# Linear attention into a top-1 expert layer: head tokens of k and v on 128 partitions, and the spill expert's weights through the sync queue

## The chip, the cores and the metric

The kernel runs on one core of a Trainium2 chip. The metric is the device time of one execution in microseconds (us). The engines are named as in the profile: PE (TensorE), DVE (VectorE), ACT (ScalarE), POOL (GpSimd) and SP (SyncE), which here only issues DMAs. All transfers run on the core's 16 DMA engines.

## The reference

Shapes: q, k, v are (8, 8, 576, 64) in float32 (batch, heads, tokens, head dim). The output is (4608, 512).

```python
kv = np.einsum('bhsd,bhse->bhde', k, v)
out = np.einsum('bhsd,bhde->bhse', q, kv)
rms = np.sqrt(np.mean(out * out, axis=-1, keepdims=True) + 1e-06)
attn = out / rms * g_norm                 # (b, h, s, d)

x = attn.transpose(0, 2, 1, 3).reshape(4608, 512)
logits = x @ w_gate                       # w_gate (512, 8)
expert_idx = np.argmax(logits, axis=1)
gate_w = softmax(logits)[row, expert_idx]
for e in range(8):                        # w1 (8, 512, 1024), w2 (8, 1024, 512)
    mask = expert_idx == e
    h = np.maximum(x[mask] @ w1[e], 0.0)
    out[mask] = gate_w[mask, None] * (h @ w2[e])
```

## The kernel before

Every instruction is put in order by hand: the program order of the Python code is the order on each engine.

**Attention.** For each batch b and half u (four heads), `load` (L541) issues three DMAs on SP's queue, one each for k, v and q, into tiles `mk`, `mv`, `mq` with four buffers each. The 128 partitions hold two heads of 64 token groups, and a group is nine tokens in a row, 576 numbers. `kv_mm` (L565) multiplies v and k of a head over 64 partitions, nine times, into the PSUM tile `kvps`; 64x64 pieces of the array work on different heads. `z_copy` (L583) takes `kvps` out, `fold_mm` (L588) multiplies by an identity beside the gate weights, and `x_copy` makes `kvx`. `t_mm` transposes q into `qT`. A tile step (`o_mm`, `o_red`, `o_nrm`, `o_x`) then makes 128 rows of attention output, their norm and their gate logits. After each group of tiles, `route` finds each row's expert and slot, and POOL scatters the rows (`xrow`) to `x_slots` in HBM.

The loop at L770 goes over b from 0 to 8. At step b it does the loads' consumers for batch b and the tiles of batch b - 1 (four tiles for odd b, five for even b); `load(b + 2, u)` follows the last transposes of a half.

**Experts.** `ffn` (L479) is a generator, of which `unit()` runs a step. Its groups, in order, are experts 0 to 2 with three tiles of 128 rows each, the same experts with two more tiles each, and experts 3 to 7 with five tiles each. An extra group for one tile, the spill, takes rows beyond five tiles of an expert; it stands before the last group. Which expert needs it is known only at run time. A group gathers its rows (`fetch`, POOL), transposes them (`xpose`), does `stage1` (w1 and relu, into `hT`) and `stage2` (w2), evicts to `y` on DVE (L351, three buffers), and scatters `y` to the output on POOL (L354). For further spill tiles a loop at the end (L837) runs a number of times that the data decide.

**Weights.** An expert's weights come in eight parts of 512 KB in float32 on SP's queue into `wst` (four buffers), and DVE casts each to float16 (`w_cast`, L204). `w_step` (L211) casts the oldest part once four are staged, then loads the next. Experts 0 to 2 may be loaded during attention (`EARLY`); the others only once the attention's memory is free (`late["pool"]`). During attention `w_step` is called twice for each b from 1 (L799) and once per tile from b = 6 (L814); in `ffn`, four times in the first stage of each group but the spill, and once for each tile of the second. The spill's weights come in another way: `dyn_group.fetch` (L380) issues twelve indirect gathers on POOL (L403) that cast on the way, by row numbers that `dyn_tables` (L421) has made on DVE.

## Time and profile before

| | |
|---|---|
| median of 3 runs | 376.94 us (373.69 to 377.51) |
| profiled execution | 376.71 us, span 374.9 us |
| granted PE clock, mean | 0.842 |
| PE busy | 292.8 us (78%) |
| DVE / ACT / POOL busy | 173.8 / 121.3 / 144.9 us |
| moved by DMA | 83.76 MB, mean 223 GB/s |
| SP's queue (q1) | 61.87 MB, 26368 packets |
| POOL's queue (q0) | 21.06 MB, 8704 packets |

The profile is of one execution. Busy shares are averages over the stages, which have different limits, so they are read stage by stage; the page cuts the span into 40 slices for that. A digit in a row of slices is the busy share in tenths. In an answer on waits, the first name is the engine that was idle, the arrow points at what released it, and the numbers are the total in us, how often, and the longest. In the chain and in the timeline, a line is the start in us, the length in us, the engine, the operation and the line of code.

### The profile page before, as it was taken

What the parts mean: (1) busy time and instruction counts of PE and PEld (TensorE: products, weight loads), DVE (VectorE), ACT (ScalarE), POOL (GpSimd) and SP (SyncE); (2) the same over time, 40 slices, a digit from 0 to 9 for tenths busy, and PEclk for the clock granted to TensorE, in tenths of its full rate; (3) what the DMA queues carried; (4) which work ended last, traced back from release to release, by engine and by line L of the source; (5) the groups of instructions that cost most, each with busy time, mean ns of one, the idle gap of its engine ahead of it and who ended that gap; (6) DMA issues with size and microseconds to landing.
All of it is one profiled execution on the core that took longest, in us unless ns stands there. A gap on an engine that the chain in (4) does not pass through costs nothing.

```text
span 374.9 us, 8180 instructions
## 1 busy us (share of the span) xinstructions
PE 292.8 (78%) x3271; PEld 202.8 (54%) x3271; DVE 173.8 (46%) x424; ACT 121.3 (32%) x324; POOL 144.9 (39%) x151
## 2 busy tenths in 40 slices
PE   2687879597948989347999979788986687998990
PEld 2476777385836778236454546445552353655640
DVE  0136355258517567576377655668701402324130
ACT  1346444155414443132431233314051041232510
POOL 7000003600352103475564447735577375413031
PEclk9999578679665566755899998989999898999996
DMA  8999999569762755582479999976528425302021
GB/s 242 391 391 392 393 395 357 215 215 376 267 255 63 206 171 198 171 250 89 141 226 394 384 388 389 373 283 224 200 78 134 132 75 70 143 28 102 3 84 50
DMA packets 36759, 83.76 MB, mean 223 GB/s; under 512 B 5740, under 2 KB 7021, under 8 KB 36720
## 3 DMA queue, kind: packets, MB, share of 16 engines
q1 hardware_dynamic: 26368, 61.87, 46.3%
q0 software_dynamic: 8704, 21.06, 17.9%
q8 instruction: 26, 0.43, 0.5%
q10 hardware_dynamic: 1648, 0.29, 0.5%
q14 instruction: 13, 0.11, 0.1%
HBM read 71.77 MB, written 15.50 MB: 233 GB/s over the span
## 4 chain that ended last, share of the span: by engine, by line
PE 45%; issue 16%; DMA 13%; DVE 11%; another core or an unknown queue 5%; ACT 4%; POOL 3%; POOLq 1%; ACTq 0%; SPq 0%; DVEq 0%
PE ops L634 11%; PE hp L330 11%; PE yp L346 8%; PE kvps L576 7%; DMA wst<-in_moe_w_dram 6%; PE tps L559 4%; POOL out_dram L354 3%; DMA mv<-in_v_dram 3%; DVE ms L647 2%; ACT sq L643 2%; PE xps L310 2%; DVE y L351 2%; DMA g<-in_g_norm_dram 2%; DVE xsT L313 1%
## 5 line engine op out<-in xcount | busy, mean ns | idle before, releaser
L338 ACT ACTIVATE hT<-hp 128x320 f16<-128x320 f32 (+3 forms) x136 | 53.5, 427 | 127.6 <-PE hp L330 105.5
L330 PE MATMUL hp<-xsT,w1e 128*128 128x320 f16 (+2 forms) x512 | 78.4, 308 | 11.7 <-DVE xsT L313 6.5
L346 PE MATMUL yp<-w2e,hT 128*128 128x512 f16 x320 | 79.0, 396 | 8.9 <-DVE y L351 5.5
L354 POOL DMA_INDIRECT out_dram<-y,idv x40 | 43.0, 1076 | 79.6 <-DVE y L351 64.9
L330 PEld LDWEIGHTS <-w1e 128*128 128x128 f16 x512 | 51.3, 100 | 38.8 <-issue 19.2
L634 PE MATMUL ops<-kvx,qT 64*128 64x72 f32 (+1 forms) x640 | 54.7, 339 | 4.4 <-issue 2.4
L346 PEld LDWEIGHTS <-hT 128*128 128x128 f16 x328 | 32.1, 102 | 43.6 <-issue 13.0
L726 POOL DMA_INDIRECT x_slots<-xrow,posi x36 | 36.3, 1007 | 46.2 <-issue 25.4
L634 PEld LDWEIGHTS ops<-kvx,qT 64*128 64x128 f32 (+1 forms) x640 | 48.3, 242 | 9.6 <-issue 4.8
L576 PE MATMUL kvps<-mk,mv 64*64 64x64 f32 x1152 | 35.4, 273 | 23.1 <-issue 12.6
L351 DVE TENSOR_SCALAR y<-yp,xl 128x512 f32<-128x512 f32 x40 | 29.9, 748 | 36.6 <-PE yp L346 29.1
L647 DVE TENSOR_REDUCE ms<-sq 128x8 f32<-128x512 f32 x36 | 24.7, 685 | 45.1 <-ACT sq L643 35.9
L576 PEld LDWEIGHTS kvps<-mk,mv 64*64 64x64 f32 x1152 | 29.5, 180 | 28.3 <-issue 27.3
L313 DVE TENSOR_SCALAR xsT<-xps,g 128x512 f16<-128x512 f16 x41 | 19.2, 477 | 45.1 <-PE xps L310 27.5
L643 ACT ACTIVATE sq<-ops 128x512 f32<-128x512 f32 x36 | 21.5, 598 | 51.6 <-PE ops L634 41.4
L276 POOL DMA_INDIRECT xl<-x_slots,idxa x31 | 32.8, 1058 | 9.4 <-issue 7.9
L693 POOL COPY xrow<-tokc 128x3 int32<-128x3 int32 x12 | 2.3, 193 | 76.3 <-DVE xrow L659 75.0
L559 PE MATMUL tps<-ctile,mq 128*128 128x128 f32 x144 | 29.3, 342 | 2.1 <-ACT qT L560 1.9
L659 DVE TENSOR_TENSOR xrow<-ops,rs 128x512 f16<-128x512 f32 x36 | 24.7, 686 | 8.8 <-ACT rs L652 8.6
L206 DVE CAST w1e<-wst 128x1024 f16<-128x1024 f32 x32 | 22.1, 706 | 11.6 <-DMA wst<-in_moe_w_dram 11.6
L206 DVE CAST w2e<-wst 128x1024 f16<-128x1024 f32 x32 | 22.4, 703 | 7.7 <-DMA wst<-in_moe_w_dram 5.8
L560 ACT COPY qT<-tps 128x384 f32<-128x384 f32 x48 | 22.2, 474 | 11.4 <-PE tps L559 11.3
(96 smaller groups left out, 186.2 us busy)
## 6 DMA issues: line engine op xcount, KB each, us to landing
wst<-in_moe_w_dram SPq DMA_DIRECT2D x64, 512.0 KB
mk<-in_k_dram SPq DMA_DIRECT2D x16, 576.0 KB
mv<-in_v_dram SPq DMA_DIRECT2D x16, 576.0 KB
mq<-in_q_dram SPq DMA_DIRECT2D x16, 576.0 KB
out_dram<-y,idv POOLq DMA_INDIRECT x40
x_slots<-xrow,posi POOLq DMA_INDIRECT x36
xl<-x_slots,idxa POOLq DMA_INDIRECT x31
xl<-x_slots,idxe POOLq DMA_INDIRECT x9
```

What stands on the lines that cost most here:

```text
L206: engine.tensor_copy(*w_staged.pop(0))
L276: nc.gpsimd.indirect_dma_start(out=self.xl[:, k, :], out_offset=None, in_=xs.ap(), in_offset=IndirectOffsetOnAxis(ap=idx[:, self.e, self.k ...
L330: nc.tensor.matmul(hp, self.w()[0][:, kk, f * 128 : (f + 1) * 128], self.xsT[:, kk, s : s + self.step], start=(kk == 0), stop=(kk == 3),)
L338: nc.scalar.activation(self.hT[:, f, s : s + self.step], hp, ACTF.Relu)
L346: nc.tensor.matmul(yp, self.hT[:, f, k * 128 : (k + 1) * 128], self.w()[1][:, f, :], start=(f == 0), stop=(f == 7),)
L351: nc.vector.tensor_scalar(y, yp, self.xl[:, k, D : D + 2].bitcast(F32), None, op0=ALU.mult)
L354: nc.gpsimd.indirect_dma_start(out=self.views(k), out_offset=IndirectOffsetOnAxis(ap=self.ids[:, k : k + 1], axis=0), in_=y, in_offset=Non ...
L559: nc.tensor.transpose(ps[:, c, :], src[:, 128 * m : 128 * m + 128], cv["ident"])
L576: nc.tensor.matmul(kvps[b][a][64 * y : 64 * y + 64, u, :], main["v", b, u][hs, y, cs], main["k", b, u][hs, y, cs], start=(c == 0), stop=(c ...
L634: nc.tensor.matmul(ps[p0 : p0 + 64 * n, y, o0 : o0 + 72], qT[b][hs, a, blk // 2 : blk // 2 + n, :].rearrange("d c p -> d (c p)"), kvx[b][h ...
L647: nc.vector.reduce_sum(mss[j, t], sq, axis=AXX)
L726: nc.gpsimd.indirect_dma_start(out=xs_views[9 * j + t0 + t], out_offset=IndirectOffsetOnAxis(ap=posi[:, t : t + 1], axis=0), in_=xrow[j, ( ...
```

## The change

Loads of k and v: each head is loaded by a DMA of its own (eight for k and v where there were two). A head now lies on all 128 partitions: partition p of the lower half holds tokens 9p to 9p + 4, partition 64 + p tokens 9p + 4 to 9p + 8, 320 numbers each. The token that lies in both is used once. q is loaded as before. `kv_mm` contracts over 128 partitions in four steps and over the upper 64 in a fifth, into one PSUM tile; `z_copy` is one copy in place of two.

The spill's weights are one more entry, "s", in the list of weight parts. SP reads the number of the expert from a table in SBUF into a register and loads the eight parts from there by that offset, and DVE casts them as for any other expert. The group for the loop at the end keeps the gathers.

The weight steps move: none up to b = 5, then one per tile for b = 6 and 7 and two for b = 8; in `ffn` none in the second stage of groups of experts 0 to 2, and two in the first stage of groups of two tiles. A group first loops until its own eight parts are cast. The tables for the spill are made in the fourth group, and `y` has five buffers in the groups of five tiles and in the spill.

```diff
-    w_todo = [(e, n) for e in range(E) for n in range(8)]
-    w_staged = []
+    w_todo = [(e, n) for e in [*range(E - 1), "s", E - 1] for n in range(8)]
+    spill_e = []
+    w_staged, w_done = [], {}
...
         st = P_wa.tile([128, F], F32, tag="wst", bufs=4, name=f"wst{e}_{n}")
+        if e == "s":
+            if n == 0:
+                spill_e.append(
+                    nc.values_load(
+                        tabs[0][5][0:1, 0:1], engines=(mybir.EngineType.SP,), min_val=0,
+                        max_val=E - 1,
+                        skip_runtime_bounds_check_because="the table holds the number of an expert",
+                    )
+                )
+            w1, w2 = (
+                w[bass.ds(spill_e[0], 1)].rearrange("o a b -> (o a) b") for w in (moe_w1, moe_w2)
+            )
+        else:
+            w1, w2 = moe_w1[e], moe_w2[e]
         if n < 4:
             r0 = 128 * (2 * (n % 2) + n // 2)
-            nc.sync.dma_start(st, moe_w1[e, r0 : r0 + 128, :])
+            nc.sync.dma_start(st, w1[r0 : r0 + 128, :])
             dst = w_tiles[e][0][:, n, :]
...
-        w_staged.append((dst, st))
+        w_staged.append((e, dst, st))
 
     def w_cast(engine):
         if w_staged:
-            engine.tensor_copy(*w_staged.pop(0))
+            e, dst, st = w_staged.pop(0)
+            engine.tensor_copy(dst, st)
+            w_done[e] = w_done.get(e, 0) + 1
...
-            y = self.pool().tile([128, D], F32, tag="y", bufs=3, name="y")
+            y = self.pool().tile([128, D], F32, tag="y", bufs=3 if self.small else 5, name="y")
...
-    class dyn_group(Group):
+    class SpillGroup(Group):
...
             self.tables, self.col, self.view = tables, col, view
-            self.e, self.K, self.n, self.step, self.small = E, 1, 128, 128, False
+            self.e, self.K, self.n, self.step, self.small = "s", 1, 128, 128, False
...
-        def slot_ids(self):
-            pass
...
         def fetch(self):
-            badi, xii, w1i, w2i, _ = self.tables
+            badi, xii, w1i, w2i = self.tables[:4]
...
+    class LoopGroup(SpillGroup):
+        def w(self):
+            return self.wd
+
+        def fetch(self):
+            super().fetch()
             self.wd = (
                 P_wa.tile([128, 4, F], F16, tag="w1e", bufs=3, name="w1d"),
...
-            yield
             for kk in range(12):
...
-                yield
-
-        def ready(self):
-            self.ids = late["pool"].tile([128, 1], I32, tag="d_id", name="d_id")
-            nc.vector.tensor_tensor(
-                self.ids, self.xl[:, 0, D + 2 : D + 4].bitcast(I32), self.ix[:, 13:14], op=ALU.max
-            )
+                    out_offset=None,
...
+        eti = small("d_eti", [128, T], I32)
+        nc.vector.tensor_scalar(eti, et, float(E - 1), None, op0=ALU.min)
...
+            while w_done.get(cur.e, 0) < 8:
+                w_step()
             for f in range(8):
                 cur.stage1(f)
-                if f % 2 == 1 and real >= 0:
+                if f % 2 == 1 if cur.K != 2 else f % 4 == 1:
                     w_step()
...
-                if f == 2 and cur.e == EARLY:
+                if f == 2 and real == EARLY:
                     tabs.append(dyn_tables())
-                if f == 0 and cur.e == EARLY + 1:
-                    spill = dyn_group(tabs[0], slice(0, 1), out_views[E * SLOT_TILES])
-                    weights = spill.fetch()
+                if f == 3 and cur.e == EARLY + 1:
+                    spill = SpillGroup(tabs[0], slice(0, 1), out_views[E * SLOT_TILES])
+                    spill.fetch()
                     order.insert(len(order) - 1, spill)
-                if cur.e > EARLY:
-                    next(weights, None)
...
-            if cur.e == E - 2:
-                for _ in weights:
-                    pass
-                spill.ready()
...
-                if real >= 0:
+                if not cur.small:
                     w_step()
...
 
         def load(b, u):
-            for n, src in (("k", k), ("v", v), ("q", q)):
-                t = PA.tile([128, 2, 576], F32, tag=f"m{n}", bufs=4, name=f"m{n}{b}{u}")
-                nc.sync.dma_start(
-                    t,
-                    src[b, 4 * u : 4 * u + 4].rearrange("(i a) (p c) d -> (a p) i (c d)", a=2, c=9),
-                )
+            for n, src in (("k", k), ("v", v)):
+                t = PA.tile([128, 4, 320], F32, tag=f"m{n}", bufs=4, name=f"m{n}{b}{u}")
+                for i in range(4):
+                    head = src[b, 4 * u + i]
+                    nc.sync.dma_start(
+                        t[:, i, :],
+                        bass.AP(
+                            tensor=head.tensor, offset=head.offset,
+                            ap=[[256, 2], [576, 64], [1, 320]],
+                        ),
+                    )
                 main[n, b, u] = t
+            t = PA.tile([128, 2, 576], F32, tag="mq", bufs=4, name=f"mq{b}{u}")
+            nc.sync.dma_start(
+                t, q[b, 4 * u : 4 * u + 4].rearrange("(i a) (p c) d -> (a p) i (c d)", a=2, c=9)
+            )
+            main["q", b, u] = t
...
         def kv_mm(b, u):
             if u == 0:
-                kvps[b] = [
-                    PSA.tile([128, 2, 64], F32, tag="KV", bufs=2, name=f"kvps{b}{a}")
-                    for a in range(2)
-                ]
-            for c in range(9):
-                cs = slice(64 * c, 64 * c + 64)
-                for y in range(2):
-                    for a in range(2):
-                        hs = slice(64 * a, 64 * a + 64)
+                kvps[b] = PSA.tile([128, 4, 64], F32, tag="KV", bufs=2, name=f"kvps{b}")
+            for a in range(2):
+                for c in range(5):
+                    hs = slice(64 if c == 4 else 0, 128)
+                    cs = slice(64 * c, 64 * c + 64)
+                    for y in range(2):
                         nc.tensor.matmul(
-                            kvps[b][a][64 * y : 64 * y + 64, u, :],
-                            main["v", b, u][hs, y, cs],
-                            main["k", b, u][hs, y, cs],
-                            start=(c == 0), stop=(c == 8),
+                            kvps[b][64 * y : 64 * y + 64, 2 * u + a, :],
+                            main["v", b, u][hs, 2 * y + a, cs],
+                            main["k", b, u][hs, 2 * y + a, cs],
+                            start=(c == 0), stop=(c == 4),
                         )
 
         def z_copy(b):
-            zs[b] = PA.tile([128, 2, 2, 64], F32, tag="z", bufs=2, name=f"z{b}")
-            for a in range(2):
-                nc.scalar.copy(zs[b][:, a], kvps[b][a])
+            zs[b] = PA.tile([128, 4, 64], F32, tag="z", bufs=2, name=f"z{b}")
+            nc.scalar.copy(zs[b], kvps[b])
...
                 xrow[j, t // 3] = PA.tile(
-                    [128, 3, ROW], I16, tag="xrow", bufs=5, name=f"xrow{j}{t}"
+                    [128, 3, ROW], I16, tag="xrow", bufs=4, name=f"xrow{j}{t}"
...
                         if x % 3 == 2:
                             if b + 2 < B:
                                 load(b + 2, x // 3)
-                            if b > 0:
-                                w_step()
...
-                if b >= B - 2:
+                for _ in range((0, 1, 1, 2)[max(b - 5, 0)]):
                     w_step()
```

## The prediction

> **What bounds the kernel now.** I read four views, in this order: the page, for the shape of the span; the DMA view of one stretch, for what the queues can carry; the waits, for who is late; the chain with its times, for where each stage ends.
>
> The page first.
>
> ```profile
> span 374.9 us, 8180 instructions
> ...
> PEclk9999578679665566755899998989999898999996
> DMA  8999999569762755582479999976528425302021
> GB/s 242 391 391 392 393 395 357 215 215 376 267 255 63 206 171 198 171 250 89 141 226 394 384 388 389 373 283 224 200 78 134 132 75 70 143 28 102 3 84 50
> ...
> q1 hardware_dynamic: 26368, 61.87, 46.3%
> q0 software_dynamic: 8704, 21.06, 17.9%
> ...
> q10 hardware_dynamic: 1648, 0.29, 0.5%
> ```
>
> Each slice is 9.4 us. The DMA engines are full twice: up to about 65 us, when k, v and q stream in, and from about 195 to 245 us, when the expert weights do. Between them TensorE is the limit, at a granted clock of five to seven tenths. The DMA view of 10 to 60 us prices the full stretch:
>
> ```profile
> DMA packets 8622, 19.62 MB, mean 392 GB/s; under 512 B 540, under 2 KB 540, under 8 KB 8613
> ...
> q1 hardware_dynamic: 8613, 19.49, 103.8%
> ```
>
> So 16 engines move 392 GB/s, 24.5 GB/s each, and one engine moves its packets without gaps from one DMA to the next (103.8% of the stretch). Now the waits, first of all engines, then of SP's queue:
>
> ```profile
> PE kvps L576 <- DMA mv<-in_v_dram: 10.3, 3, 7.3
> ```
> ```profile
> SPq L544 <- PE kvps L576: 24.4, 6, 10.6
> ```
>
> TensorE waits for k and v only three times, all at the start. Later SP waits for TensorE: the loads run ahead and are held back by their four buffers. The chain gives the ends of the stages:
>
> ```profile
> 143.01 2.13 PE kvps L576 x72
> ...
> 173.80 0.76 DVE xsT L313 x2
> ...
> 176.33 2.72 PE hp L330 x8
> ```
> ```profile
> 289.20 3.50 another core or an unknown queue
> 292.73 0.76 DVE y L351
> ```
>
> The last kv product starts at 143 us, although SP issued its loads by 98 us; the first expert matmul starts at 176.3. That leaves 374.9 - 176.3 = 198.6 us for the experts. The second fence of the chain is one of the places where the expert stage stalls: an eviction to y (three buffers) waits for something that the chain can't name. I read it as the scatter that would free the buffer, which stands on POOL's queue behind the spill group's weight gathers (seven of the twelve are issued from 281 to 288 us).
>
> [...]every DMA of q1 has 128 partitions outermost on both sides, and rows (48 x 256 for k, v, q; 32 x 128 and 32 x 256 for the weights: 24,576) plus 16 completions for each of 112 issues (1,792) make the 26,368 packets of the page. No DMA of the kernel before has a smaller outer dimension[...].
>
> **The change part by part.**
>
> *Loads of k and v.* The pattern before merges heads and token groups into one dimension of 128. The new one, per head, is [[256, 2], [576, 64], [1, 320]]: the outer dimension is 2, since a step of 256 can't merge with 64 steps of 576. [...]Per engine a head is 64 rows of 1,280 bytes. The price of such a row: at 24.5 GB/s, 52 ns; by a line through two rows of the page, q1 (46.3% of 16 x 374.9 us over 26,368 packets = 105 ns for 2,346 bytes) and q10 (0.5%: 18 ns for 176 bytes), 62 ns. I take 56, nearer the first, because packets overlap a little when an engine is full (the 103.8%). [...]There are 8 x 8 heads of k and as many of v: 128 x 64 = 8,192 rows on each of the two engines, 459 us[...]. Behind them in the same queue stand q's rows: 16 loads x 16 rows x 94 ns (2,304 bytes at 24.5 GB/s) = 24 us. POOL's scatters of x share the two engines: about 24 of 36 come before the end, 132 KB / 16 = 8.3 KB at 123 ns per 2.4 KB (q0) = 0.42 us each, 10 us. With 2 us before the first issue moves data, the last of k, v, q lands at 2 + 459 + 24 + 10 = 495 us, where before it was needed at 143. SP issues nine DMAs for three, 96 more at about 0.4 us: 38 us on SP, beside 459 of transfer, nothing. Bytes go up by a ninth (320 for 288); that is in the row price.
>
> *The kv products.* 16 calls of 72 records become 40 records on 128 rows. At full clock 72 took 1.28 us (chain, 18.90 us), four 64x64 tiles at once; on 128 rows only two can go at once, so one call costs 0.7 (same time per record) to 1.4 us (twice). At most 9 us gained or 2 lost over the kernel, and all of it lies beside the loads: nothing. The same holds for one copy of z in place of two and the row buffers of four for five.
>
> *Weight steps.* Before, 14 steps (two for each b from 1) and then one per tile from b = 6, 28 in all, which is enough for all 24 loads of the early experts. After: none up to b = 5, then 5 + 4 + 10 = 19. On SP they now stand behind the last k, v, q, so the first arrives at about 495 us; 19 x 0.524 MB at 390 GB/s is 26 us, beside the remaining attention. The first cast (DVE, fifth step, end of b = 6) waits for that too, and evictions and reductions of b = 6 and 7 queue behind it on DVE, hence TensorE behind its two O buffers. So I count the stretch from the last kv product to the first expert matmul whole: 176.3 - 143.0 = 33 us (25, since TensorE's clock was low there before, to 45).
>
> *Experts.* POOL loses twelve gathers (0.94 to 0.96 us and 0.3 between them, 15 us); y gets five buffers; DVE gets eight casts more (0.70 us, 5.6 us in all) and SP eight loads. Casts move out of the small groups: 3 x 4 + 3 x 2 = 18 steps for 3 x 7 + 3 x 6 = 39. From the timeline, undisturbed groups take 11.5 us (three tiles), 8.3 (two), 19 (five), 6.7 (spill), and 9.4 us follow the last matmul: 3 x 11.5 + 3 x 8.3 + 5 x 19 + 6.7 + 9.4 = 171 for 198.6. Still to load are 53 of 72 parts, 28 MB, 71 us at 390 GB/s, which fits but leaves less slack in the small groups, where a group now loops until its own weights are cast. I take 180 (171 to 200). SP's new wait, for the table that names the spill expert, comes with step 57; behind it stand the spill loads and those of expert 7; the table is made in the fourth group, by step 40, so nobody waits.
>
> Sum: 495 + 33 + 180 = 708 of span, and 1.8 us around it (376.71 - 374.9): **710 us**. The profiled execution lies within 0.3 us of the median of 376.94, so no further correction. The bounds added: [...]2 + 508 + 24 + 10 + 45 + 200 + 2 = 791.
>
> **The rivals.**
>
> *Sixteen engines all the same* (the other side): the split falls on the 64 rows or on the partitions. For it: every issue before used 16[...]. Then a unit is 1.90 MB for 1.77, 4.9 us at 390 GB/s, SP's nine issues of 0.4 us fit under it, and the nine weight loads of the first 100 us (12 us of transfer) move out. Attention stays TensorE's: 174; experts 180; with 2 around it 356 us. It decides from the point where the stream takes under 143 us: 918 us of rows / k + 34, so from k = 9 up (16 in practice).
>
> *More than two, fewer than that,* or pairs that are taken in turn but don't overlap fully: at k = 4, 266 + 33 + 180 + 2 = 481 us. For it speaks only that the trace can't show the assignment.
>
> *Sixteen engines, but weights late:* 53 loads for 40 are 17 us more in a stage that was DMA-full for 50 us; if the small groups wait for all of it and the y gain is small, 377 + 17 - 9 = 385. Against it: big groups have room, 9 steps of 1.3 us in 19.
>
> **How the numbers follow.** Two engines 0.84; sixteen 0.10; between 0.03; weights late 0.03. The first case's bounds are 588 to 791; I give 600 to 790, which leaves out little of it, and with the other cases about 2 in 10. A difference of about 1% is what a measurement here tells from none. Faster: 0.10 (all of the sixteen-engine case); within 1%: 0.02, from the edges of that case and the late weights; slower: 0.88.
>
> **What would show it.** Right: the page's DMA row at 1 and 45 to 50 GB/s for two thirds of the span; q1 with 35,968 packets (34,304 rows, 2 completions for each of 128 issues, 16 for 88) in place of 37,760; kvps waiting for mv for hundreds of us; heads landing some 3.6 us apart. Experts: no L403 on POOL, and 171 to 200 us from the first hp to the end. Wrong: full DMA slices at the start and the last kvps before 150 us.

## The result: 702.0 us for 377.2 us, and the profile after

The changed kernel takes 702.04 us (median of 4 runs, 697.1 to 704.16); the kernel before, in the same comparison, 377.23 us. The ratio is 1.865, with a 95% interval of 1.8475 to 1.8825. It is slower, by nearly the amount forecast (710 us). Ratios here and below compare only runs in the faster of the two states that executions show, while medians are of all runs, so the two can differ by up to 2%. The kernel before itself took 343 to 381 us on the chips of the three sets of experiments; so times are compared only within a set, where all kernels ran on one chip.

The page of the changed kernel (each slice of its rows is 17.6 us):

```profile
span 702.4 us, 7326 instructions
...
PEclk9999999985555555555555555555579999999987
DMA  2212212212124121221312212174697665888901
GB/s 56 78 49 79 78 49 79 76 52 79 50 79 134 55 78 50 79 78 62 126 49 92 85 50 79 50 226 149 201 323 258 230 223 205 285 306 307 341 7 72
...
q1 hardware_dynamic: 35968, 68.16, 28.6%
```

Where the row of bytes began at 242 to 395 GB/s, it now begins at 49 to 79 and stays at that level, but for four slices, until 456 us, the 26th slice of 40. A DMA share of one to two tenths of 16 engines, at 49 GB/s, is two engines at the 24.5 GB/s that one of them moved before. The queue has 35,968 packets: 34,304 rows, and only two completions for each of the 128 loads of a head. TensorE is late where it never was:

```profile
PE kvps L596 <- DMA mv<-in_v_dram: 281.1, 45, 21.0
```

281.1 us of waiting for v, in 45 waits, for 10.3 us in three. SP's own timeline (start, length, operation) shows how the loads come in. These are the issues of the last half batch, and the first weights after it:

```profile
427.74 11.84 SPq L559 DMA_DIRECT2D mk<-in_k_dram  x4
439.62 13.00 SPq L559 DMA_DIRECT2D mv<-in_v_dram  x4
452.73 3.14 SPq L568 DMA_DIRECT2D mq<-in_q_dram  x1
455.91 2.62 SPq L208 DMA_DIRECT2D wst<-in_moe_w_dram  x4
```

An issue of k or v took 0.44 us before (the median; 1.6 at most); now one holds SP for 3.2 us. In the test of loads alone, below, an issue takes 3.2 us where two engines are at work, 1.6 with four, and 0.6 with eight or sixteen; what SP waits for is not shown. Eight heads and one q take 28.2 us (424.5, the q before, to 452.73, start to start), and there are 16 such halves. The DMA view of 452 to 470 us, in slices of 0.45 us, shows when the last of them landed:

```profile
GB/s 51 46 51 51 48 48 51 46 51 51 166 212 348 378 329 298 298 349 280 307 322 315 347 313 311 348 330 408 275 101 64 46 55 46 55 73 55 114 127 405
```

For 4.5 us two engines work (46 to 51 GB/s). Then the other fourteen fill with weights, and when these are done, from about 465 us, the row is back at 46 to 73: the two engines are still at what was queued on them, heads first and their share of the weights last. So I put the landing of the last k, v, q at about 464 us. (In a run of the third set the last product waits for nothing but its data, and starts 7.6 us after the last issue of q ends; here that would be at 463.5.) The first weight part is whole at 467. DVE's timeline shows who stood still in the meantime:

```profile
418.31 0.69 DVE L666 TENSOR_REDUCE ms<-sq 128x8 f32<-128x512 f32 x1 [1.31 <-ACT sq L662]
467.01 0.69 DVE L222 CAST w1e<-wst 128x1024 f16<-128x1024 f32 x1 [48.02 <-DMA wst<-in_moe_w_dram]
```

The first cast of a weight part came in DVE's order at 419 us and waited 48 us for a part that stood behind the last k, v, q on SP's queue. TensorE's timeline has the echo:

```profile
470.74 0.23 PE L722 MATMUL rps<-ohb,h 128*128 128x56 f16 x1 [30.40 <-DVE ohb L710]
...
473.00 2.99 PE L596 MATMUL kvps<-mk,mv 128*64 128x64 f32 x40
```

The routing product `rps` waits for `ohb`, which stands behind the cast on DVE, and the kv product stands behind `rps` on TensorE. So the last kv product starts some 9 us after its data. The chain then gives the first expert matmul (`hp` is the tile of `stage1`):

```profile
514.98 2.73 PE hp L347 x8
```

The span divides into 464 us of stream, 51 us to the first expert matmul, and 702.4 - 515.0 = 187.4 us of experts.

### The profile page after: what moved, and what is told of

The parts are those of the page before. It is cut to its first block, busy times and chain, and to the rows that moved or that the text cites. A ratio compares the mean times of both kernels' runs of the same rounds, so it can differ in the third digit from the quotient of the medians.

```text
span 702.4 us, 7326 instructions
## 1 busy us (share of the span) xinstructions
PE 343.4 (49%) x2759; PEld 242.9 (35%) x2759; DVE 181.3 (26%) x433; ACT 122.9 (17%) x316; POOL 135.9 (19%) x139
## 3 DMA queue, kind: packets, MB, share of 16 engines
q1 hardware_dynamic: 35968, 68.16, 28.6%
## 4 chain that ended last, share of the span: by engine, by line
SPq 62%; PE 11%; issue 9%; DMA 7%; POOL 5%; DVE 5%; another core or an unknown queue 1%; POOLq 0%; ACT 0%; DVEq 0%
SPq L559 55%; SPq L568 7%; PE hp L347 5%; DMA out_dram<-y,d_id 3%; PE yp L363 3%; POOL out_dram L371 3%; DMA mv<-in_v_dram 2%; DMA wst<-in_moe_w_dram 2%; POOL xl L293 2%; PE ops L653 1%; DVE w2e L222 1%; DVE ms L666 1%; PE xps L327 1%; DVE xrow L678 1%
## 5 line engine op out<-in xcount | busy, mean ns | idle before, releaser
L596 PE MATMUL kvps<-mk,mv 128*64 128x64 f32 (+1 forms) x640 | 61.3, 326 | 281.1 <-DMA mv<-in_v_dram 281.1
L596 PEld LDWEIGHTS kvps<-mk,mv 128*64 128x64 f32 (+1 forms) x640 | 47.7, 216 | 295.1 <-issue 157.4
L347 PE MATMUL hp<-xsT,w1e 128*128 128x320 f16 (+2 forms) x512 | 80.2, 312 | 11.4 <-DVE xsT L330 6.2
L363 PE MATMUL yp<-w2e,hT 128*128 128x512 f16 x320 | 75.9, 385 | 0.0
L653 PE MATMUL ops<-kvx,qT 64*128 64x72 f32 (+1 forms) x640 | 68.2, 401 | 6.8 <-DVE lhat L682 5.9
L653 PEld LDWEIGHTS ops<-kvx,qT 64*128 64x128 f32 (+1 forms) x640 | 61.1, 300 | 13.2 <-issue 9.7
L371 POOL DMA_INDIRECT out_dram<-y,idv x40 | 44.7, 1117 | 79.9 <-DVE y L368 68.0
L582 PE MATMUL tps<-ctile,mq 128*128 128x128 f32 x144 | 38.1, 426 | 0.8 <-ACT qT L583 0.6
L605 ACT COPY z<-kvps 128x256 f32<-128x256 f32 x8 | 3.0, 372 | 162.4 <-PE kvps L596 162.4
L582 PEld LDWEIGHTS tps<-ctile,mq 128*128 128x128 f32 x144 | 25.7, 214 | 6.6 <-ACT qT L583 2.9
```

The costliest lines, as they stand in the source:

```text
L347: nc.tensor.matmul(hp, self.w()[0][:, kk, f * 128 : (f + 1) * 128], self.xsT[:, kk, s : s + self.step], start=(kk == 0), stop=(kk == 3),)
L363: nc.tensor.matmul(yp, self.hT[:, f, k * 128 : (k + 1) * 128], self.w()[1][:, f, :], start=(f == 0), stop=(f == 7),)
L371: nc.gpsimd.indirect_dma_start(out=self.views(k), out_offset=IndirectOffsetOnAxis(ap=self.ids[:, k : k + 1], axis=0), in_=y, in_offset=Non ...
L582: nc.tensor.transpose(ps[:, c, :], src[:, 128 * m : 128 * m + 128], cv["ident"])
L596: nc.tensor.matmul(kvps[b][64 * y : 64 * y + 64, 2 * u + a, :], main["v", b, u][hs, 2 * y + a, cs], main["k", b, u][hs, 2 * y + a, cs], st ...
L653: nc.tensor.matmul(ps[p0 : p0 + 64 * n, y, o0 : o0 + 72], qT[b][hs, a, blk // 2 : blk // 2 + n, :].rearrange("d c p -> d (c p)"), kvx[b][h ...
```

## Experiments

Theory T: the loads of single heads run on two engines, and that is the whole loss; the rest of the change gains somewhat. Its rival in size, R: the loads cost something else as well (more issues, shorter rows, the 128-row product), so that the layout would be slow on sixteen engines too.

### First set: the parts alone, and the outer dimension

**The same bytes with 64 outermost.** Only the order of the loads' dimensions changes: token groups outermost, the four heads of a half inside, one DMA for each half of the partitions. Tiles, layout and products stay.

```diff
-                for i in range(4):
-                    head = src[b, 4 * u + i]
+                head = src[b, 4 * u]
+                for r in range(2):
                     nc.sync.dma_start(
-                        t[:, i, :],
+                        t[64 * r : 64 * r + 64],
                         bass.AP(
-                            tensor=head.tensor, offset=head.offset,
-                            ap=[[256, 2], [576, 64], [1, 320]],
+                            tensor=head.tensor, offset=head.offset + 256 * r,
+                            ap=[[576, 64], [36864, 4], [1, 320]],
```

> Same tiles, same rows of 1,280 bytes, same bytes and same products as the changed kernel; only the pattern is turned: two DMAs for each of k and v per half (one for each half of the partitions), with the 64 token groups outermost and the four heads inside. Theory A (the outer dimension of 2 confines each DMA to two engines): the stream spreads over 16 engines, attention is TensorE's again at about 174 us, experts as in the changed kernel 187, together about 363 us (350 to 372). Theory B (short rows or many small DMAs are what costs): the rows are the same, so about 700 us stays. Theory C (SP needs its time for each issue): half as many issues for k and v, about 480 us.

Measured: 382.13 us (380.77 before on this chip), ratio 1.0197 (1.0144 to 1.0251). The 0.865 of loss is gone but for 0.02, with the same bytes at the same partitions. That is T. But it is not the 363 us expected, and R has its part. The DMA view of 12 to 60 us:

```profile
DMA packets 8263, 11.58 MB, mean 241 GB/s; under 512 B 486, under 2 KB 6726, under 8 KB 8259
...
q1 hardware_dynamic: 8259, 11.52, 109.0%
```

All sixteen engines are busy (109.0%), and yet 241 GB/s come for the 392 of before. And the products got longer, as the groups of TensorE's instructions show (busy us and mean ns of one after the bar; then idle time). This kernel first, then the third of this set, which keeps the products of before:

```profile
L596 PE MATMUL kvps<-mk,mv 128*64 128x64 f32 (+1 forms) x640 | 45.1, 299 | 17.5 <-DMA mv<-in_v_dram 14.6 <-issue 2.8
```

```profile
L589 PE MATMUL kvps<-mk,mv 64*64 64x64 f32 x1152 | 34.9, 267 | 21.1 <-issue 12.4 <-DMA mv<-in_v_dram 8.5
```

640 records take 10 us more than 1,152. The first expert matmul is at 194.6 of 374.0 us here and at 176.5 of 356.2 in that third kernel, so attention takes 18 us more, and the experts take the same (179.4 and 179.7). What the layout costs on sixteen engines lies in attention, and it is about what the rest of the change gains. Both losses are taken up in the second set.

**Loads alone.** The kernel before with the new loads, and the products, the copy of z and the four row buffers that go with them. Weight steps and the spill's weights stay as they were.

```diff
-                t = PA.tile([128, 2, 576], F32, tag=f"m{n}", bufs=4, name=f"m{n}{b}{u}")
+                t = PA.tile([128, 4, 320], F32, tag=f"m{n}", bufs=4, name=f"m{n}{b}{u}")
+                for i in range(4):
...
+                            ap=[[256, 2], [576, 64], [1, 320]],
```

> The kernel before with only the loads of k and v, the products and the copy of z changed (and four row buffers, so that it fits); weight steps, spill and y buffers as before. If the loads are the whole loss: the stream takes 455 us as in the changed kernel, plus 14 weight parts that now stand in the same queue (33 KB each on each of the two engines, 1.3 us, 19 us), then 35 to 45 us to the first expert matmul and 199 us for the experts as before: 710 to 730 us, somewhat slower than the changed kernel. If the rest of the change had a share in the loss, it comes out below 690.

Measured: 732.69 us, ratio 1.9186 (1.9075 to 1.9298), just above what was expected. So the loads are more than the whole loss, and the rest of the change takes some 0.05 in the ratio back. The last q is issued at 468.6 us here, 16 us later than in the changed kernel, since weight steps stand between the loads as before; the first expert matmul is at 529.7 us.

**The rest alone.** The changed kernel with the loads, products and z of before.

```diff
-            for n, src in (("k", k), ("v", v)):
-                t = PA.tile([128, 4, 320], F32, tag=f"m{n}", bufs=4, name=f"m{n}{b}{u}")
...
+            for n, src in (("k", k), ("v", v), ("q", q)):
+                t = PA.tile([128, 2, 576], F32, tag=f"m{n}", bufs=4, name=f"m{n}{b}{u}")
```

> The changed kernel with the loads of k and v, the products and the copy of z put back as before; weight steps, spill weights through SP and five y buffers stay. If the rest is a gain that the loads buried: attention 174 to 177, experts 183 to 190, about 363 us (355 to 370). If the rest is neutral or harmful by itself (weights late for the small groups): 377 us or more.

Measured: 361.72 us (median of four) against 380.8 us before on this chip, inside the 355 to 370 expected. These four runs give no interval, so it was taken up again in the third set. Its profile has the first expert matmul at 176.5 of 356.2 us, so 179.7 us of experts, for the 180 of the prediction and the 198.6 of before.

**The loads by themselves.** No computation: sixteen loads of a head (eight in the last stage), then a small copy on DVE that ends the stage. The outer dimension of the source goes 2, 4, 8, 16, 128; then 2 again from two queues by turns (SP and ACT), and 2 with rows of 2,304 bytes.

```diff
+    ("outer2", "s", [[256, 2], [576, 64], [1, 320]]),
+    ("outer4", "s", [[192, 4], [1152, 32], [1, 320]]),
+    ("outer8", "s", [[192, 8], [2304, 16], [1, 320]]),
+    ("outer16", "s", [[192, 16], [4608, 8], [1, 320]]),
+    ("outer128", "s", [[256, 128], [1, 320]]),
+    ("outer2_two_queues", "sa", [[256, 2], [576, 64], [1, 320]]),
+    ("outer2_long_rows", "s", [[256, 2], [512, 64], [1, 576]]),
```

> Loads alone, without any of the computation: seven stages one after another, each loading 16 heads of k (2.62 MB in rows of 1,280 bytes) with an outer dimension of 2, 4, 8, 16 and 128, then of 2 with the issues alternating between the queues of SP and ACT, then eight loads with an outer dimension of 2 and rows of 2,304 bytes (2.36 MB). Theory A, with k the outer count[...]: 49, 98, 196, 350 to 390 and 350 to 390 GB/s, that is 53, 27, 13.5, 7 and 7 us and about 2 us more for each stage; two queues still 49 GB/s, since they share the two engines; long rows 49 to 51 GB/s, 46 to 48 us. If pairs were taken in turn, two queues would give about 98 GB/s. Theory B (short rows): all five alike, and long rows clearly faster. Theory C (SP's issue time): two queues twice as fast as one, and the outer count without effect.

Measured, in DVE's timeline (the copy starts when the stage's loads have landed; the wait in brackets is the stage's length):

```profile
56.33 0.18 DVE L44 COPY res<-big 128x16 f32<-128x16 f32 x1 [54.94 <-DMA big<-in_k_dram]
86.13 0.18 DVE L44 COPY res<-big 128x16 f32<-128x16 f32 x1 [29.62 <-DMA big<-in_k_dram]
102.94 0.18 DVE L44 COPY res<-big 128x16 f32<-128x16 f32 x1 [16.64 <-DMA big<-in_k_dram]
116.13 0.18 DVE L44 COPY res<-big 128x16 f32<-128x16 f32 x1 [13.01 <-DMA big<-in_k_dram]
127.98 0.18 DVE L44 COPY res<-big 128x16 f32<-128x16 f32 x1 [11.68 <-DMA big<-in_k_dram]
184.44 0.18 DVE L44 COPY res<-big 128x16 f32<-128x16 f32 x1 [56.27 <-DMA big<-in_k_dram]
233.16 0.17 DVE L44 COPY res<-big 128x8 f32<-128x8 f32 x1 [48.55 <-DMA big<-in_k_dram]
```

54.9, 29.6 and 16.6 us for 2, 4 and 8: the same 2.62 MB, in steady slices 49, 98 and 196 GB/s, so 24.5 GB/s for each engine, the figure of before. A row of 1,280 bytes is then 52 ns, not 56. So in these three values the outer dimension of the source is the number of engines at work, as the prediction had assumed for 2. With 128 outermost the same sixteen loads, with the same rows, take 11.7 us for 54.9, so neither the row length nor the number of loads is the cause. From 16 up the stage no longer doubles its speed, and the 350 to 390 GB/s expected there were not reached. At 16, SP's issues follow one another without a wait, 0.6 us each, about 10 of the 13 us, so I take SP to be the limit; at 128 an issue takes 0.43 us, and what limits that stage stays open. Rows of 2,304 bytes on two engines give about 51 GB/s: long rows hardly help. The stage with two queues, in the DMA view of 128 to 184.4 us:

```profile
DMA packets 2080, 2.62 MB, mean 46 GB/s; under 512 B 32, under 2 KB 2080, under 8 KB 2080
...
q1 hardware_dynamic: 1040, 1.31, 6.5%
q10 hardware_dynamic: 1040, 1.31, 6.3%
```

Half of the packets are on each queue, their time is 12.8% of sixteen engines, which is two, and the stage takes 56.3 us for the 54.9 of one queue. So both queues use the same two engines, and splitting the stream over these two queues doesn't get around the limit.

### Second set: why sixteen engines are still slow, and the wait of the weights

**Weight steps only at b = 8.** A test of the stretch from the last load to the first expert matmul, for which the prediction had 33 us: no step at b = 6 and 7, four per tile at b = 8, so that no cast stands ahead of the reductions of b = 6 and 7.

```diff
-                for _ in range((0, 1, 1, 2)[max(b - 5, 0)]):
+                for _ in range((0, 0, 0, 4)[max(b - 5, 0)]):
```

> The changed kernel with no weight step at b = 6 and 7 and four for each tile of b = 8 (20 in place of 19). In the changed kernel DVE stood 48 us at the first weight cast, which waits behind the last k, v and q, and with it the tiles of b = 7. If that wait is what stretches the end of attention (59 us from the last issue of q to the first expert matmul, where the kernel before needed 33 from its last kv product): 35 to 45 us, total 680 to 690. If the stretch is only routing and a slow TensorE clock: 700 to 704 as before.

Measured: 686.01 us, ratio 2.0018 (1.9888 to 2.0149) on a chip where before took 342.9; the total expected was meant for a chip where it takes 377, so only the stretch is a test. From the end of the last q's issue (457.4) to the first expert matmul (510.1) are 53 us, for 59 in the changed kernel, profiled on another chip. DVE's wait of 48 us is gone, and the last kv product starts 9 us after the last issue (at 466.4), not 17; but sixteen casts are now pressed into the tiles of b = 8. Waits for weight parts make 34% of the chain from 440 to 520 us, and 20 us of them stand between the last kv product and the first expert matmul. One wait was traded for several. The expectation (35 to 45 us) failed.

**All 128 partitions in each load.** Tokens 0 to 511 as four tokens on each of the 128 partitions, rows of 1,024 bytes, all four heads in one DMA; the last 64 tokens in rows of 256 bytes on the upper 64 partitions. The products are those of the change.

```diff
-                for i in range(4):
...
+                        ap=[[256, 128], [36864, 4], [1, 256]],
...
+                nc.sync.dma_start(
+                    t[64:128, :, 256:320],
...
+                        ap=[[64, 64], [36864, 4], [1, 64]],
```

> The changed kernel with k and v loaded by patterns whose outer count is 128 and 64: tokens 0 to 511 as four in a row on each of 128 partitions (rows of 1,024 bytes, all four heads in one DMA), tokens 512 to 575 one on each of the upper 64 partitions (rows of 256 bytes). The products stay on 128 partitions. Sixteen engines and all partitions in the large DMA. The earlier run with outer 64 moved only 241 GB/s in the full stretch, where the kernel before moved 392. Theory H (each of its DMAs wrote to half of the partitions, and that halves what can land): here the stream is back at 350 GB/s or more, attention ends 9 to 13 us later than with the loads of before (16 products at 0.5 to 0.8 us more each), total 364 to 372. Theory S (rows of 1,280 bytes and less cost that much on sixteen engines whatever the partitions): still 230 to 260 GB/s, total 374 to 384.

Measured: 355.06 us, ratio 1.0228 (1.0124 to 1.0332). The stream is faster than with 64 outermost (DMA view, 12 to 60 us), though not at the 350 expected:

```profile
DMA packets 15658, 14.72 MB, mean 307 GB/s; under 512 B 5024, under 2 KB 13584, under 8 KB 15653
```

TensorE waits for v only 9.2 us in all, and the kernel is no nearer to the one before. So at this point the stream is not what the 2% hang on.

**The rest alone, with three y buffers.** As the third kernel of the first set, and `y` as before.

```diff
-            y = self.pool().tile([128, D], F32, tag="y", bufs=3 if self.small else 5, name="y")
+            y = self.pool().tile([128, D], F32, tag="y", bufs=3, name="y")
```

> The kernel with the rest of the change alone (loads and products as before), but with three y buffers again. The rest alone took about 358 us. If the y buffers matter: the eviction stalls of the large groups come back in part, 364 to 372. If taking the twelve gathers off POOL is enough by itself, since the scatters then leave on time: 356 to 361.

Measured: 334.93 us, ratio 0.9663 (0.955 to 0.9776). The times expected were meant for the chip of the first set, so the question of the y buffers is left to the third. The first expert matmul is at 157.0 us, where the kernel with loads on all 128 partitions, otherwise the same but for the y buffers, has it at 183.2. These 26 us, where 9 to 13 were expected, are the price of the layout in attention on sixteen engines; the experts give 6 of them back (174.7 us for 180.4; why was not looked into), so that the two kernels differ by 20 us (355.06 and 334.93). In attention TensorE is busy 38 us longer and idle 12 us less. Its groups (`ops` is the product of a tile step), of the kernel with 128-row products first:

```profile
L659 PE MATMUL ops<-kvx,qT 64*128 64x72 f32 (+1 forms) x640 | 63.7, 385 | 2.5 <-DVE lhat L688 2.5
L602 PE MATMUL kvps<-mk,mv 128*64 128x64 f32 (+1 forms) x640 | 45.5, 313 | 9.2 <-DMA mv<-in_v_dram 9.2
```

```profile
L647 PE MATMUL ops<-kvx,qT 64*128 64x72 f32 (+1 forms) x640 | 52.2, 327 | 8.4 <-DVE lhat L676 5.7 <-issue 2.7
...
L589 PE MATMUL kvps<-mk,mv 64*64 64x64 f32 x1152 | 28.8, 265 | 11.9 <-DMA mv<-in_v_dram 8.3 <-issue 3.6
```

The products take 16.7 us more, and `ops`, which the change doesn't touch, 11.5 more for the same 640 records; the transposes of q another 7.3 (36.5 for 29.2). TensorE runs these at two speeds. Sixteen records of `ops`, in the timelines of the two kernels in the same order:

```profile
24.41 1.98 PE L659 MATMUL ops<-kvx,qT 64*128 64x72 f32 x16
28.63 1.99 PE L659 MATMUL ops<-kvx,qT 64*128 64x72 f32 x16
...
89.11 1.12 PE L659 MATMUL ops<-kvx,qT 64*128 64x72 f32 x16
```

```profile
22.57 1.11 PE L647 MATMUL ops<-kvx,qT 64*128 64x72 f32 x16
26.71 1.12 PE L647 MATMUL ops<-kvx,qT 64*128 64x72 f32 x16
```

1.98 or 1.11 us for the same work. With the new products TensorE is at the slow speed for all of its attention but 89 to 107 us; with the old ones for about half of it. A whole call of the products has 2.99 or 1.82 us (40 records, 128 rows) for 2.20 or 1.28 (72 records, 64 rows): at either speed the new form is longer, by 0.8 or 0.5 us. So of the 26 us, some 9 to 13 (16 calls) are the products themselves, and the rest is the slower speed. Why TensorE is held at it with the new products was not tried and stays open.

The starts of the single records, in the traces of the kernel before and of the one with loads on all 128 partitions, show where a call of the new form loses its time. At the fast speed the old records start in fours, 59 ns apart, and the new ones in pairs, 58 ns apart: that alone would be 20 pairs for 18 fours. But the fifth step has 64 rows for the 128 of the others. At each of the three changes of rows in a call the pairs stand 155 to 158 ns apart, and after the first pair of a call and the pair behind each change 107. Together this is 0.5 us of the 1.82, and about 0.65 of the 2.99 at the slow speed. A form without the change of rows was not tried.

**What half the partitions cost a load.** Loads alone again, each with four heads of k: 128 partitions; two DMAs of 64 partitions each from one queue; the same from two queues; then rows of 1,024 bytes, rows of 256 bytes on 64 partitions, and rows of 2,304 bytes.

```diff
+    ("p128_rows1280", 128, "s", [[256, 128], [36864, 4], [1, 320]]),
+    ("p64_rows1280", 64, "s", [[576, 64], [36864, 4], [1, 320]]),
+    ("p64_two_queues", 64, "sa", [[576, 64], [36864, 4], [1, 320]]),
+    ("p128_rows1024", 128, "s", [[256, 128], [36864, 4], [1, 256]]),
+    ("p64_rows256", 64, "s", [[64, 64], [36864, 4], [1, 64]]),
+    ("p128_rows2304", 128, "s", [[576, 128], [73728, 2], [1, 576]]),
```

> Loads alone again, without any of the computation: six stages of eight loads of four heads. In order: 128 partitions with rows of 1,280 bytes (5.24 MB); the same bytes as twice as many DMAs to 64 partitions, lower and upper half in turn; the same with the lower halves from SP's queue and the upper from ACT's; 128 partitions with rows of 1,024 bytes (4.19 MB); 64 partitions twice over with rows of 256 bytes (1.05 MB); 128 partitions with rows of 2,304 bytes (4.72 MB). Theory H (half the partitions, half the rate): 370 to 390, about 240, again 350 or more when both halves are in flight at once, 350 to 380, well under 200, 390 GB/s; that is 14, 22, 15, 12, 6 and 12 us, and about 2 more for each stage. Theory S (short rows): the first three stages alike at about 240 GB/s, and the fourth lower still.

Measured, the copies on DVE that end the first three stages, of 5.24 MB each:

```profile
29.45 0.17 DVE L48 COPY res<-big 128x8 f32<-128x8 f32 x1 [17.39 <-DMA big<-in_k_dram]
54.94 0.17 DVE L48 COPY res<-big 128x8 f32<-128x8 f32 x1 [25.32 <-DMA big<-in_k_dram]
75.57 0.17 DVE L48 COPY res<-big 128x8 f32<-128x8 f32 x1 [20.46 <-DMA big<-in_k_dram]
```

17.4 us on 128 partitions and 25.3 on 64 at a time; in steady slices 363 and 233 GB/s. The DMA view of the second stage (29.5 to 54.9 us) tells that no engine stood idle:

```profile
DMA packets 4352, 5.24 MB, mean 206 GB/s; under 512 B 256, under 2 KB 4352, under 8 KB 4352
...
q1 hardware_dynamic: 4352, 5.24, 97.1%
```

All sixteen are busy, for 97.1% of the stage, and each packet takes longer: 91 ns in the mean, for 59 on 128 partitions (4,224 packets at 89.5% of 17.4 us). This agrees with the 241 GB/s of the kernel with 64 outermost; why packets take longer there is not shown. When the two halves come from two queues at once, the rate climbs from some 235 to about 355 GB/s in the middle of the stage, with as many DMAs of the same size, so neither their number nor their size is the cause; why it starts low is open, and the whole stage takes 20.5 us where 17 were expected. On 128 partitions shorter rows cost little: 389 GB/s at 2,304 bytes, 363 at 1,280 and about 350 at 1,024. The stage with rows of 256 bytes hangs on its sixteen issues of 0.6 us, about 10 of its 12.5 us, and doesn't price such rows.

### Third set: the gain of the rest, and the early weights

**The rest alone, again, in five rounds.**

> The rest of the change alone once more, for an interval: loads of k and v, products and copy of z as before, everything else as changed (five y buffers). Experts stage 180 us where the kernel before has 199, attention the same: ratio to the kernel before 0.94 to 0.96. If it had only been the chip of that run: 0.98 to 1.02.

Measured: 369.6 us, ratio 0.9741 (0.9626 to 0.9856). It is a gain, but smaller than the 0.94 to 0.96 expected.

**The same with three y buffers.**

> The same with three y buffers, on the same chip as the one with five, since the two were run on different chips before. With three buffers 0.966 of the kernel before was measured. If the fourth and fifth y buffer do nothing once the gathers are off POOL: the same time within 1%. If they matter: 1 to 3% slower than with five.

Measured: 367.64 us, ratio 0.973 (0.9622 to 0.9838). So five buffers gain nothing over three once the gathers are off POOL. They do what they are for: with three, the waits have this line, which with five is gone:

```profile
DVE y L368 <- DMA out_dram<-y,idv: 5.1, 6, 1.5
```

But the scatters are no longer behind weight gathers on POOL, the longest such wait is 1.5 us, and nothing hangs on it. Against the kernel before on the same chip, these two kernels are the fastest of all that were run.

**The changed kernel again**, as the measure for the next one.

> The changed kernel itself, on the same chip as the next run. The stream of k, v and q doesn't depend on TensorE's clock: SP's last issue of q ends at 456 us as before (454 to 459). On a chip where the kernel before takes 377 us: 702; where it takes 343, about 690.

Measured: 702.14 us, ratio 1.8731 (1.8568 to 1.8894). The last q's issue ends at 455.3 us, the first expert matmul is at 513.7 (58.4 later), and DVE waits 48.0 us in one piece for a weight part, as in the first profile.

**Early weights.** The 24 parts of the early experts are loaded, and all but the last four cast, from b = 1 to 4, three steps per half batch, so that no cast is left in b = 6 and 7; one step per tile at b = 8.

```diff
+                            for _ in range(3 if 0 < b < 5 else 0):
+                                w_step()
...
-                for _ in range((0, 1, 1, 2)[max(b - 5, 0)]):
+                for _ in range((0, 0, 0, 1)[max(b - 5, 0)]):
```

> The changed kernel with the 24 early weight parts loaded three per half at b = 1 to 4 instead of from b = 6, and one cast step per tile of b = 8. The parts then stand among the k and v loads in SP's queue and have all landed long before the end; each costs the two busy engines 8 rows of 4,096 bytes, 1.3 us, 32 us in all, so SP's last issue of q ends at 480 to 492 us for 456. If DVE's wait for parts behind the last k and v, and the casts packed into the end, are what stretched the end of attention (59 us from the last issue of q to the first expert matmul in the changed kernel, 53 with all steps at b = 8): 33 to 42 us here, so that the total stays within 1.5% of the changed kernel. If routing and TensorE's half clock are the reason: 50 to 59 us here too, and a total about 25 us longer.

Measured: 720.12 us, ratio 1.9199 (1.904 to 1.9358). The last q's issue ends at 498.4 us, and the first expert matmul is at 537.1: 38.7 us for 58.4, in the expected 33 to 42. TensorE's timeline shows why, with the last product of b = 7 waiting for its data and for nothing else:

```profile
506.01 1.50 PE L596 MATMUL kvps<-mk,mv 128*64 128x64 f32 x18 [1.74 <-DMA mv<-in_v_dram]
```

From there to the first expert matmul are 31 us, what the prediction took from the profile of before (33). So DVE's wait for the weights and the casts after it are 20 us of the stretch: this is shown. The stream pays for it, 43 us in place of the 25 to 37 expected, because each weight part also needs its turn on the two engines: at the 1.3 us estimated for a part (8 rows of 4,096 bytes on each, at 24.5 GB/s), 24 parts account for 32 us, and the other 11 stay open. So the total, expected within 1.5% of the changed kernel, is 2.6% longer. On the two profiles: +43 for the stream, -20 for the stretch, -7 for the experts (179.2 for 185.9), +17 in all (span 716.3 for 699.6).

## Why the prediction was right, step by step

- **Two engines.** That an outer dimension of 2 would put a load on two engines was not shown by the trace of before, where every load on SP's queue has 128 outermost; it was the author's assumption, at 0.84, and the k of the rivals is this number of engines. Now it is shown: 35,968 packets as counted beforehand, 49 GB/s where only heads are loading, and the ladder over 2, 4 and 8. With 64 outermost the loss goes from 0.865 to 0.02 of the time before. The rival of pairs that are taken in turn (481 us) is out.
- **The row's price.** 56 ns was taken between 52 and 62; the trace has 52. 8,192 rows are then 426 us for 459, 33 less, and the last k, v, q lands at about 464 us for 495. The error is wholly in this term: I gave weight to a line through two rows of the page, which mixes busy and quiet engines, where the rate of a full engine (24.5 GB/s) was at hand and right. The lower bound of 588 us for the sum had a shorter time for a row, which was not shown.
- **From the last load to the experts.** 33 us were predicted and 51 measured from the landing. The prediction named the wait (DVE's first cast, behind the last k, v, q), and yet gave it no time of its own: it took the stretch from before whole, as if the last product could start with its data. It started some 9 us late, and then the casts of 15 of the 19 parts, none of which had come before, were in DVE's order between the reductions: 42 us from product to expert for 33. The run with early weights takes 20 us of this away.
- **Experts.** 180 predicted, 187.4 measured in the changed kernel, 179.7 to 185.7 with the loads of before; inside the bounds of 171 to 200. One part of the reasoning fails: the prediction counted five y buffers among the gains, and with the gathers off POOL they add nothing to three. What is left is these gathers (the trace has no gather of weights on POOL any more) and the place of the weight steps; the two were not separated.
- **The kv products.** Bounded at 9 us gained to 2 lost; they lose 0.5 to 0.8 us a call, 9 to 13 in all. The bound of 1.4 us ("twice") for a call failed: it takes 1.82 at the fast speed. That only two tiles go at once was right, and the records show it (pairs, 58 ns apart at the fast speed); what the estimate left out are the changes between 128 and 64 rows, 0.5 us, and the slower speed in place of the fast one. It cost nothing here, since it lies beside the loads, as the prediction had it.
- **The other side.** On sixteen engines 356 us were given, a gain of 6%. With the loads spread it is a loss of 2% in both ways that were tried, so lifting the limit of two engines alone doesn't bring the gain. The rival kept "attention stays TensorE's: 174" and 390 GB/s, and neither holds: the first expert matmul came at 194.6 and 183.2 us, the full stretch ran at 241 and 307 GB/s. Its 180 us of experts do hold (179.4 and 174.7).

The sum's errors are -31, +18 and +7 us on the span, which leave the forecast 6 us too high. The cause is shown. That the size fits to 1% is partly luck: the errors cancel. One line was misread without harm to the sum: between the two full stretches the page's clock row has not only fives to sevens, but also an eight and a nine.

## What to carry to other kernels

Before a layout is changed for the engines' sake, look at the outermost dimension of the access pattern on the memory side of its loads. Here 2 gave 49 GB/s with rows of 1,280 bytes and 51 with rows of 2,304, the rate of two engines, and 64 outermost, with the bytes and tiles as they were, took the loss from 0.865 to 0.02 of the time before. Let each DMA reach all 128 partitions too (363 GB/s here, 233 on 64). Where an engine works in program order, an instruction that waits for a DMA stops all that is behind it (48 us on DVE here), so the place of a cast is set by what stands ahead of its transfer in the queue. And a contraction over twice as many rows is no gain by itself (1.82 us a call here for 1.28): price a whole call against the smaller tiles that run side by side, with the steps that have fewer rows.

## What the runs showed of the hardware that I had not expected

- Loads with an outer dimension of 2 from two queues at once share the same two engines: 56.3 us for 54.9 from one.
- Loads of 64 partitions from one queue keep all sixteen engines busy (97.1% of the stage) and yet run at 233 GB/s in its steady part, for 363 on 128 partitions.
- SP is held 3.2 us for each issue of a head while two engines carry the loads, 1.6 us with four, and 0.6 with eight or sixteen.
- A kv product over 128 rows takes 1.82 or 2.99 us a call, four 64x64 tiles over 64 rows 1.28 or 2.20. Each change between records of 128 and 64 rows within a call costs it about 0.15 us at the fast speed (100 ns at the change, 49 behind the next pair).
- TensorE takes 1.98 us for work that takes 1.11 at other times, and the page's row of the granted clock doesn't always tell: with loads on all 128 partitions it reads 9 in the slices from 24 to 81 us, where all of these `ops` have the slow time. The durations of equal instructions are the surer sign.
